# Newton's steps of the layer norm in the batch passes: from VectorE to Pool

## The chip, the core and the metric

The kernel runs on one core of a Trainium2 chip. The core has a matrix engine (TensorE, PE in the profile), a vector engine (VectorE, DVE), an activation engine (ScalarE, ACT), a general engine (GpSimd, POOL) and an engine that issues the transfers here (SyncE, SP). The engines run their own instruction streams side by side and wait for one another through semaphores. The metric is the device time of one execution in microseconds. The kernel before takes 328.29 us, the median of three runs (327.77 to 330.49).

## What is computed

Two layers of a decoder step for four batch entries (B = 4, one token each, D = 512). Each layer is an attention block over a cached K and V (32 query heads, 8 K/V heads, 4096 positions, head size 128) and a gated block (F = 1792), each behind a layer norm and with a residual. Both layers use the same caches and weights, all bfloat16.

```python
def _layernorm(x, axis=-1, eps=1e-5):
    m = jnp.mean(x, axis=axis, keepdims=True)
    v = jnp.var(x, axis=axis, keepdims=True)
    return (x - m) / jnp.sqrt(v + eps)

def _A_ref(x, k_cache, v_cache, wq, wo):
    q = (x @ wq).reshape(B, 1, 32, 128).transpose(0, 2, 1, 3)
    k = jnp.repeat(k_cache, 4, axis=1); v = jnp.repeat(v_cache, 4, axis=1)
    p = softmax(jnp.einsum("bhqd,bhkd->bhqk", q, k) * 128 ** -0.5)
    o = jnp.einsum("bhqk,bhkd->bhqd", p, v)
    return o.transpose(0, 2, 1, 3).reshape(B, 1, 4096) @ wo

def _B_ref(x, w_gate, w_up, w_down):
    h = sigmoid(x @ w_gate) * (x @ w_up)
    return h @ w_down

x = A_x
for _ in range(2):
    x = x + _A_ref(_layernorm(x), ...)
    x = x + _B_ref(_layernorm(x), ...)
```

## The kernel before

**Blocks and slots.** The caches are read in blocks of 1 MB, one per layer, batch entry and K/V head, for K and V alike. Twelve slots in SBUF hold them. SP issues a load as soon as the planned next load has a free slot (`pump`, L332), and some blocks of layer 0 are kept for layer 1. Freed slots, by the last product that reads a block, therefore set when the loads start.

**Steps.** The main loop (L1146) takes two heads per step, 32 steps in all, and each step also does the V products of the step before: scores on PE (`scores`, L910), the row maximum on DVE (`smax`, L926), its spread over the rows on PE (`spread_max`, L935), the bias on DVE (L945) and the exponential on ACT (L953), the transposes of the next K blocks on DVE (`k_turn`, L893), the V products on PE (`pv`, L1018), their scaling on DVE (L1046), the turn of the probabilities (`ptrans`, L970 on PE and 16 copies of L1002 on ACT), and the output projection (`wo_pair`, L1062 on PE, L1076 on DVE). Every engine takes its instructions in the order in which the program hands them out; there is no planner, and `_Sched` (L34) only adds the semaphore waits from the names that each instruction reads and writes. A wait is also set between two dependent instructions of one engine.

**Passes.** When a batch entry has finished its attention of layer 0, a pass takes it through the gated block and on to the query of layer 1 (`pass_steps`, L859). There are four, one per entry, and the list `places` (L1102) says after which part of which step each of the 19 parts of a pass is handed out. A pass has two halves, and each begins with a layer norm: `ln_a` (mean, centred x), `ln_b_sum` (sum of squares on PE, L550), `ln_b_rs` (L555).
- `ln_b_rs` reduces the sum on DVE (L558, from PSUM), forms variance plus eps (L565, `vpe`) and a first guess of the inverse root from its bits (L570, `y0i`), and for one entry calls `newton_one` (L503): three Newton steps, each two instructions on one column of 128 rows (L507 and L515), the last of which writes `rs`.
- First half: gate row on PE (`gate_row`, L709), `gate_tanh` (the scale `rsg` from `rs` on DVE, L721; the tanh on ACT, L726), `up_row` (L738), `up_gate` (copy on ACT, L749; product on DVE, L751), `h_turn` (L762 on PE, L768 on DVE), `down` (L828) and `down_add` (L841, L851).
- Second half: query rows on PE (`q_row`, L779, twice), `q_out(0)` (ACT, L792, scaled by `rs`), `q_half(0)` on PE (L809), `q_out(1)` (DVE, L799, scaled by `rs`), `q_turn` (L809, L818), `q_spread` (L620 on PE, L631 on ACT).

In DVE's order, Newton's steps of the first half stand between the row maximum (L926) and the bias (L945) of the same step, the gate's scale right behind that bias and ahead of a K transpose; Newton's steps of the second half stand ahead of the row maximum of their step.

**Pool.** Pool forms the query blocks of each step (`q_blocks`, L645), one product of 128 x 128 elements, and nothing else after the start. For the first heads of a batch entry in layer 1, `q_blocks` comes after the end of that entry's pass.

The start (L1086) and the end (L1194) do the layer norm for all four entries at once; there `ln_b_rs` calls `newton_many`.

Of the kernel before, what the change touches and what calls it, by code (L numbers as in the profile page):

```python
# [7 lines left out]
ALU = mybir.AluOpType  # L8
# [107 lines left out]
def bass_interleave_layers__gqa_block_cached__glu_gated_glu__decode_kernel(  # L116
# [41 lines left out]
    S = _Sched()  # L158
# [40 lines left out]
    lnsum, lnsq, vpe, nt_a, nt_b, nt_c, nt_y, rs = [newt[:, i, :] for i in range(8)]  # L199
# [154 lines left out]
    def dve(fn, reads=(), writes=()):  # L354
        return S.inst("dve", fn, reads=reads, writes=writes)

    def act(fn, reads=(), writes=()):
        return S.inst("act", fn, reads=reads, writes=writes)

    S.dma("sp", lambda e: e.dma_start(x_io[0:Bn, :], A_x.rearrange("b s d -> (b s) d")), "xin", writes=["row0"])  # L360
    for k in range(KD):
# [4 lines left out]
            writes=[f"wq{k}"],  # L366
# [6 lines left out]
        reads=["ones_f"],  # L373
        writes=["pe0"],
    )
    dve(lambda e: e.transpose(pidx[:, :], iota_f[:, 0:32]), writes=["pe0"])
    for a in range(4):
# [5 lines left out]
            reads=["pe0"],  # L383
            writes=[f"ident{a}"],
# [5 lines left out]
    for k in range(KD):  # L390
# [12 lines left out]
        reads=["M0"],  # L403
        writes=[f"x{b}" for b in range(Bn)],
# [62 lines left out]
    def ln_a(b0, nb):  # L467
# [22 lines left out]
            writes=["xc"],  # L490
        )
        act(
            lambda e: e.activation(xc_bf[:, :, 0:nb], xc_sb[:, :, 0:nb], ACTF.Copy),
            reads=["xc"],
# [8 lines left out]
    def newton_one(y0):  # L503
        y, yk = y0, "y0i"
        for it, three in enumerate((3.0, 12.0, 768.0)):
            dve(
                (lambda y: lambda e: e.scalar_tensor_tensor(  # L507
                    out=nt_a[:, 0:1], in0=y, scalar=vpe[:, 0:1], in1=y, op0=ALU.mult, op1=ALU.mult
                ))(y),
                reads=[yk, "vpe"],  # L510
                writes=["nt_a"],
            )
            z, zk = ((nt_b[:, 0:1], "nt_b"), (nt_c[:, 0:1], "nt_c"), (rs[:, 0:1], "rs"))[it]
            dve(
                (lambda y, z, three: lambda e: e.scalar_tensor_tensor(  # L515
                    out=z, in0=nt_a[:, 0:1], scalar=-three, in1=y, op0=ALU.add, op1=ALU.mult
                ))(y, z, three),
                reads=[yk, "nt_a"],
                writes=[zk],
            )  # L520
            y, yk = z, zk

    def newton_many(y0, nb):
        y, yk = y0, "y0i"
        for it, three in enumerate((3.0, 12.0, 768.0)):
            dve(
                (lambda y: lambda e: e.tensor_tensor(nt_a[:, 0:nb], y, y, ALU.mult))(y),
                reads=[yk],
                writes=["nt_a"],
            )  # L530
            dve(
                lambda e: e.tensor_tensor(nt_y[:, 0:nb], nt_a[:, 0:nb], vpe[:, 0:nb], ALU.mult),
                reads=["nt_a", "vpe"],
                writes=["nt_y"],
            )
            z, zk = ((nt_b[:, 0:nb], "nt_b"), (nt_c[:, 0:nb], "nt_c"), (rs[:, 0:nb], "rs"))[it]
            dve(
                (lambda y, z, three: lambda e: e.scalar_tensor_tensor(
                    out=z, in0=nt_y[:, 0:nb], scalar=-three, in1=y, op0=ALU.add, op1=ALU.mult
                ))(y, z, three),  # L540
                reads=[yk, "nt_y"],
                writes=[zk],
            )
            y, yk = z, zk
# [10 lines left out]
    def ln_b_rs(nb):  # L555
        M = M_ps[1]
        dve(
            lambda e: e.tensor_reduce(  # L558
                lnsq[:, 0:nb], M[:, 32:32 + KD * nb].rearrange("p (k b) -> p b k", k=KD), AX.X, ALU.add
            ),  # L560
            reads=["M1"],
            writes=["lnsq"],
        )
        dve(
            lambda e: e.tensor_scalar(vpe[:, 0:nb], lnsq[:, 0:nb], inv_d, eps, op0=ALU.mult, op1=ALU.add),  # L565
            reads=["lnsq"],
            writes=["vpe"],
        )
        dve(
            lambda e: e.tensor_scalar(  # L570
                y0i[:, 0:nb], vpe[:, 0:nb].bitcast(dt.int32), -0.5, RSQRT_MAGIC, op0=ALU.mult, op1=ALU.add
            ),
            reads=["vpe"],
            writes=["y0i"],
        )
        y0 = y0i[:, 0:nb].bitcast(dt.float32)
        if nb == 1:
            newton_one(y0)
        else:
            newton_many(y0, nb)  # L580

    def ln_b(nb):
        ln_b_sum(nb)
        ln_b_rs(nb)
# [29 lines left out]
    def q_spread(b0, nb):  # L614
        N = HQ * nb
        fns = []
        for t in range(NT4):
            for a in range(4):
                fns.append(
                    (lambda t, a: lambda e: e.matmul(  # L620
                        M_ps[1][32 * a:32 * a + 32, t * N:(t + 1) * N],
                        lhsT=ident_bf[:, bass.ds(64 * (t // 2) + t % 2, 32, step=2)],
                        rhs=qT_sb[:, 0:N],
                        start=True,
                        stop=True,
                    ))(t, a)
                )
        S.group("pe", fns, reads=["qT"] + IDENT, writes=["M1"])
        for bi in range(nb):
            act(  # L630
                (lambda bi: lambda e: e.activation(  # L631
                    qc_sb[:, b0 + bi, :, :, :],
                    M_ps[1][:, 0:NT4 * N].rearrange("p (t u r b) -> p u t r b", t=NT4, u=HKV, r=REP)[:, :, :, :, bi],
                    ACTF.Copy,
                ))(bi),
                reads=["M1"],
                writes=[f"qc{b0 + bi}"],
            )
# [16 lines left out]
    def gate_up(nb, which):  # L655
# [14 lines left out]
        if which == 0:  # L670
            dve(
                lambda e: e.tensor_tensor(
                    gs_sb[:, 0:KF * nb].rearrange("p (k b) -> p k b", k=KF),
                    M[:, 64:64 + KF * nb].rearrange("p (k b) -> p k b", k=KF),
                    bc(rs[:, 0:nb], KF, nb),
                    ALU.mult,
                ),
                reads=["M0", "rs"],
                writes=["pe0"],
            )  # L680
            act(
                lambda e: e.activation(t_sb[:, 0:KF * nb], gs_sb[:, 0:KF * nb], ACTF.Tanh, scale=0.5 * RS),
                reads=["pe0"],
                writes=["pe0"],
            )
        else:
            dve(
                lambda e: e.scalar_tensor_tensor(
                    out=hT_bf[:, :, 0:nb],
                    in0=t_sb[:, 0:KF * nb].rearrange("p (k b) -> p k b", k=KF),  # L690
                    scalar=1.0,
                    in1=M[:, 64:64 + KF * nb].rearrange("p (k b) -> p k b", k=KF),
                    op0=ALU.add,
                    op1=ALU.mult,
                ),
                reads=["pe0", "M1"],
                writes=["qT"],
            )
# [18 lines left out]
        S.group("pe", fns, reads=["xcb"] + wkeys["wg"], writes=["M0"])  # L717

    def gate_tanh():
        dve(  # L720
            lambda e: e.tensor_scalar(rsg, rs[:, 0:1], 0.5 * RS, None, op0=ALU.mult),  # L721
            reads=["rs"],
            writes=["rsg"],
        )
        act(
            lambda e: e.activation(M_ps[0][:, :], M_ps[0][:, :], ACTF.Tanh, scale=rsg),  # L726
            reads=["rsg"],
            writes=["M0"],
        )
# [129 lines left out]
    def pass_steps(b0):  # L859
        return [  # L860
            lambda: ln_a(b0, 1),
            lambda: ln_b_sum(1),
            lambda: ln_b_rs(1),
            gate_row,
            gate_tanh,
            up_row,
            up_gate,
            h_turn,
            lambda: down(b0, 1),
            lambda: down_add(b0, 1),  # L870
            lambda: ln_a(b0, 1),
            lambda: ln_b_sum(1),
            lambda: ln_b_rs(1),
            lambda: q_row(0),
            lambda: q_out(0),
            lambda: q_row(1),
            lambda: q_out(1),
            q_turn,
            lambda: q_spread(b0, 1),
        ]  # L880
# [380 lines left out]
```

## Time and profile before

| | |
|---|---|
| median of three runs | 328.29 us (327.77 to 330.49) |
| the profiled execution | 326.9 us, of which the profiled span is 325.1 us |
| PE busy | 224.6 us (69%) |
| DVE busy | 190.3 us (59%), 443 instructions |
| ACT busy | 146.0 us (45%) |
| POOL busy | 12.8 us (4%), 36 instructions |
| read from memory | 120.85 MB, 372 GB/s over the span |
| mean granted PE clock | 0.71 of full speed |

A span is the time between the first and the last instruction of one profiled execution; 1.8 us of that execution lie around it. A group row gives the line, the engine, the operation, what is written and read with its shape, the count, the busy time, the mean duration of one instruction, and how long its engine sat idle just before such instructions and for whom. A row of the chain of work that ended last gives a start, a duration and the work that the end depended on in that stretch. A window row gives, for one stretch of time, the busy share and number of instructions of PE, PE's weight loads, DVE, ACT and POOL, the granted clock, the busy share of the transfer engines and what they moved.

### The profile page before, as it was taken

The page shows a single profiled execution, that of the slowest core. Times are in us where ns is not written, and L with a number is a line of the kernel's source. Part 1 is how long each engine was busy: PE and PEld are TensorE (multiplying, and loading weights), DVE is VectorE, ACT ScalarE, POOL GpSimd, SP SyncE. Part 2 cuts the span into 40 slices and gives each one's busy share as a digit, 9 for nine tenths or more (in the row PEclk, how much of TensorE's full clock was granted, in tenths as well). Part 3 has the DMA queues.
Part 4 walks back from the last instruction along what each step waited for, and adds up shares of the span by engine and source line. Part 5 has one row for each costly group of instructions (what it writes and reads, how often), then busy time and mean ns, then how long its engine had stood idle before and what let it go on. Part 6 is the DMA issues. An engine that isn't in the chain of part 4 may idle for free.

```text
span 325.1 us, 10423 instructions
## 1 busy us (share of the span) xinstructions
PE 224.6 (69%) x4408; PEld 156.7 (48%) x4408; DVE 190.3 (59%) x443; ACT 146.0 (45%) x600; POOL 12.8 (4%) x36
## 2 busy tenths in 40 slices
PE   1345514322298988859699885979977778988975
PEld 1313312221166556636556653665555556455865
DVE  6387333331566566876544986664996567475443
ACT  1005412303046367654637664462766454377620
POOL 0000000000000000000001000000100000010000
PEclk9999999999999955555675555566555557655555
DMA  7999999999999899999989999999999999899700
GB/s 280 428 419 410 400 404 402 401 382 392 401 414 391 347 409 422 421 418 361 382 299 390 420 422 420 418 423 416 417 418 421 417 357 386 331 390 415 296 2 5
DMA packets 22526, 121.53 MB, mean 374 GB/s; under 512 B 1992, under 2 KB 7888, under 8 KB 8912
## 3 DMA queue, kind: packets, MB, share of 16 engines
q1 hardware_dynamic: 22480, 120.86, 92.5%
q8 instruction: 35, 0.57, 0.7%
q14 instruction: 11, 0.09, 0.1%
HBM read 120.85 MB, written 0.00 MB: 372 GB/s over the span
## 4 chain that ended last, share of the span: by engine, by line
DMA 32%; PE 27%; issue 20%; SPq 11%; DVE 8%; POOL 0%; ACT 0%; DVEq 0%; POOLq 0%
DMA slot<-in_A_v_cache_dram 32%; PE O_ps L1018 8%; SPq L352 6%; PE S_ps L910 6%; SPq L338 4%; DVE slot L893 4%; PE MS L935 2%; PE O_ps L1062 2%; PE MS L977 2%; PE M_ps L828 1%; DVE small L926 1%; PE PT L970 1%; PE M_ps L779 1%; PE M_ps L661 1%; PE M_ps L473 1%
## 5 line engine op out<-in xcount | busy, mean ns | idle before, releaser
L893 DVE STREAM_TRANSPOSE slot<-slot 128x2048 f32<-128x2048 f32 (+1 forms) x63 | 114.8, 1822 | 41.8 <-DMA slot<-in_A_k_cache_dram 41.8
L1002 ACT ACTIVATE pT<-PT 32x64 bf16<-32x64 f32 x504 | 108.5, 215 | 61.4 <-PE PT L970 49.8
L1018 PE MATMUL O_ps<-pT,slot 128*128 128x4 bf16 x2048 | 63.0, 166 | 37.5 <-DMA slot<-in_A_v_cache_dram 36.8
L1018 PEld LDWEIGHTS O_ps<-pT,slot 128*128 128x128 bf16 x2048 | 64.4, 105 | 41.0 <-DMA slot<-in_A_v_cache_dram 40.3
L910 PE MATMUL S_ps<-slot,qz 128*16 128x512 bf16 x512 | 59.2, 610 | 3.3 <-POOL qz L645 2.7
L953 ACT ACTIVATE pe<-S_ps,small 128x512 bf16<-128x512 f32 x32 | 22.0, 687 | 69.3 <-issue 36.4
L935 PE MATMUL MS<-valid_f,small 128*128 128x64 f32 x64 | 20.2, 415 | 32.2 <-DVE small L926 32.2
L935 PEld LDWEIGHTS MS<-valid_f,small 128*128 128x128 f32 x64 | 14.7, 286 | 45.5 <-DVE small L926 42.2
L1062 PEld LDWEIGHTS O_ps<-oT,wo 128*128 128x128 bf16 x640 | 19.3, 105 | 12.9 <-issue 12.4
L926 DVE TENSOR_REDUCE small<-S_ps 128x1 f32<-128x512 f32 x32 | 21.2, 663 | 7.0 <-PE S_ps L910 7.0
L645 POOL TENSOR_TENSOR qz<-qc,small 128x128 bf16<-128x128 bf16 x32 | 12.6, 401 | 281.1 <-ACT qc L631 148.2
L910 PEld LDWEIGHTS S_ps<-slot,qz 128*16 128x16 bf16 x512 | 12.3, 108 | 22.5 <-issue 17.5
L1062 PE MATMUL O_ps<-oT,wo 128*128 128x2 bf16 (+1 forms) x640 | 20.2, 165 | 1.2 <-issue 0.9
L1046 DVE TENSOR_TENSOR oT<-O_ps,rden 128x8 bf16<-128x8 f32 x32 | 5.2, 164 | 23.2 <-PE O_ps L1018 21.4
L977 PE MATMUL MS<-head_f,small 128*128 128x8 f32 x64 | 17.6, 348 | 0.0
L977 PEld LDWEIGHTS MS<-head_f,small 128*128 128x128 f32 x64 | 16.1, 309 | 0.0
L985 DVE RECIPROCAL rden<-MS 128x8 f32<-128x8 f32 x32 | 6.6, 206 | 13.2 <-PE MS L977 13.2
L970 PE MATMUL PT<-ident_bf,pe 128*128 128x64 bf16 x128 | 11.7, 230 | 1.7 <-ACT pe L953 1.7
L945 DVE CUSTOM_DVE_ANT_0 junk<-MS,mask_f,small 128x64 bf16<-128x64 f32 x32 | 8.5, 265 | 7.3 <-PE MS L935 7.3
L779 PE MATMUL M_ps<-wq,xc_bf 128*1 128x512 bf16 x128 | 12.6, 563 | 0.0
L473 PE MATMUL M_ps<-xT,small 128*128 128x4 f32 (+1 forms) x20 | 5.8, 362 | 5.6 <-DVE xT L851 2.2
L550 PEld LDWEIGHTS M_ps<-sq,small 128*128 128x128 f32 x20 | 5.0, 312 | 8.4 <-issue 6.8
(79 smaller groups left out, 144.1 us busy)
## 6 DMA issues: line engine op xcount, KB each, us to landing
slot<-in_A_v_cache_dram SPq DMA_DIRECT2D x53, 1024.0 KB, 10.9
slot<-in_A_k_cache_dram SPq DMA_DIRECT2D x49, 1024.0 KB, 11.5
wq<-in_A_wq_dram SPq DMA_DIRECT2D x4, 1024.0 KB, 7.8
wo<-in_A_wo_dram SPq DMA_DIRECT2D x8, 512.0 KB, 16.2
wg<-in_B_w_gate_dram SPq DMA_DIRECT2D x4, 448.0 KB, 14.1
wu<-in_B_w_up_dram SPq DMA_DIRECT2D x4, 448.0 KB, 14.5
wd<-in_B_w_down_dram SPq DMA_DIRECT2D x2, 896.0 KB, 16.5
row<-in_A_x_dram SPq DMA_DIRECT2D x1, 4.0 KB
```

The costliest lines, as they stand in the source:

```text
L352: S.dma("sp", (lambda dst, src: lambda e: e.dma_start(dst, src))(dst, src), f"d{s}", writes=[f"s{s}"])
L779: (lambda k, st: lambda e: e.matmul(M_ps[h][32 * st:32 * st + 1, :], lhsT=xc_bf[:, k, 0:1], rhs=wv[:, k, h, :, st, :], start=(k == 0), sto ...
L893: dve(lambda e: e.transpose(kf, kf), writes=[f"s{st}"])
L910: (lambda t, b2, e_, c, r0, ul: lambda e: e.matmul(S_ps[p][r0:r0 + 4 * REP, :], lhsT=qz_sb[p][:, ul, t, :, :].rearrange("p a r -> p (a r)" ...
L926: lambda e: e.tensor_reduce(rm_sb[p], S_ps[p][:, :], AX.X, ALU.max),
L935: lambda e: e.matmul(MS[:, 0:16 * REP], lhsT=rm_sb[p].broadcast_to([P, P]), rhs=valid_f[:, :], start=True, stop=True),
L953: lambda e: e.activation(pe_sb[p].rearrange("p j m -> p (j m)"), S_ps[p][:, :], ACTF.Exp, bias=nm_sb[p], scale=exp_scale, accum_out=sm_sb[ ...
L970: (lambda j: lambda e: e.matmul(PT[:, j * 64:(j + 1) * 64], lhsT=pe_sb[p][:, j, :], rhs=valid_bf, start=True, stop=True))(j)
L977: lambda e: e.matmul(MS[:, 64:64 + 2 * REP], lhsT=sm_sb[p].broadcast_to([P, P]), rhs=head_f[:, :], start=True, stop=True),
L1002: (lambda dst, frm: lambda e: e.activation(dst, frm, ACTF.Copy))(dst, frm),
L1018: (lambda x, c, j: lambda e: e.matmul(O_ps[p][:, ul * REP:(ul + 1) * REP], lhsT=vv[:, x * JG + c * 4 + j, :], rhs=pT_sb[p][:, x, j, 2 * ul ...
L1062: (lambda c, r: lambda e: e.matmul(O_ps[p][:, 64 + 2 * c:64 + 2 * c + nb], lhsT=wo_sb[:, u * REP + r, c * P:(c + 1) * P], rhs=oT_sb[n][:, ...
```

## The change

In the four passes, variance, first guess, Newton's six operations and the gate's scale are handed to Pool instead of DVE. DVE's `scalar_tensor_tensor` becomes Pool's `tensor_scalar` with the second tensor as a column scalar, so that each half step stays one operation. The reduce L558 stays on DVE, as do the layer norms of all four entries at the start and the end (`nb` is 4 there).

```diff
+    def pool(fn, reads=(), writes=()):
+        return S.inst("pool", fn, reads=reads, writes=writes)
+
...
     def newton_one(y0):
         y, yk = y0, "y0i"
         for it, three in enumerate((3.0, 12.0, 768.0)):
-            dve(
-                (lambda y: lambda e: e.scalar_tensor_tensor(
-                    out=nt_a[:, 0:1], in0=y, scalar=vpe[:, 0:1], in1=y, op0=ALU.mult, op1=ALU.mult
+            pool(
+                (lambda y: lambda e: e.tensor_scalar(
+                    nt_a[:, 0:1], y, y, vpe[:, 0:1], op0=ALU.mult, op1=ALU.mult
                 ))(y),
...
-            dve(
-                (lambda y, z, three: lambda e: e.scalar_tensor_tensor(
-                    out=z, in0=nt_a[:, 0:1], scalar=-three, in1=y, op0=ALU.add, op1=ALU.mult
+            pool(
+                (lambda y, z, three: lambda e: e.tensor_scalar(
+                    z, nt_a[:, 0:1], -three, y, op0=ALU.add, op1=ALU.mult
                 ))(y, z, three),
...
-        dve(
+        eng = pool if nb == 1 else dve
+        eng(
             lambda e: e.tensor_scalar(vpe[:, 0:nb], lnsq[:, 0:nb], inv_d, eps, op0=ALU.mult, op1=ALU.add),
...
-        dve(
+        eng(
             lambda e: e.tensor_scalar(
                 y0i[:, 0:nb], vpe[:, 0:nb].bitcast(dt.int32), -0.5, RSQRT_MAGIC, op0=ALU.mult, op1=ALU.add
             ),
...
     def gate_tanh():
-        dve(
+        pool(
             lambda e: e.tensor_scalar(rsg, rs[:, 0:1], 0.5 * RS, None, op0=ALU.mult),
```

## The prediction

> **What bounds the kernel now.** I read the chain that ended last first, since busy shares mix stages with different limits. Its totals, then pieces of it in order of time (start us, us, what):
>
> ```profile
> DMA 32%; PE 27%; issue 20%; SPq 11%; DVE 8%; POOL 0%; ACT 0%; DVEq 0%; POOLq 0%
> ```
> ```profile
> 245.53 16.36 DMA slot<-in_A_v_cache_dram
> 261.93 1.01 PE O_ps L1018 x32
> ...
> 272.98 0.58 DVE row L751
> 273.70 0.25 PE M_ps L762 x4
> ...
> 279.49 3.39 PE M_ps L779 x31
> 282.88 0.19 PE M_ps L809 x4
> ...
> 322.74 0.68 DVE row L1215
> ```
>
> Up to 261.9 us the chain keeps coming back to V blocks: the cache stream sets the time, and a delay in computing counts only if it starves that stream. After 261.9 no transfer is left on the chain: the fourth pass (264 to 286 us) and all behind it are computing, so a delay there reaches the end whole.
>
> The other passes start at about 92, 148 and 206 us. Whether they starve the stream is read from one-microsecond windows (last two columns: DMA share, GB/s):
>
> ```profile
> 107.00:108.00 1.00, 1.00 (x10) 0.55 (x14) 0.47 (x3) 0.00 (x0) 0.00 (x0) 1.00 0.70 172
> 108.00:109.00 1.00, 1.00 (x20) 0.33 (x16) 0.85 (x5) 0.00 (x0) 0.00 (x0) 1.00 0.51 131
> ...
> 164.00:165.00 1.00, 1.00 (x14) 0.41 (x17) 0.62 (x4) 0.00 (x0) 0.00 (x0) 0.50 0.50 98
> ...
> 222.00:223.00 1.00, 1.00 (x16) 0.32 (x12) 0.90 (x5) 0.10 (x1) 0.00 (x0) 0.50 1.02 426
> ```
>
> Passes 1 and 2 already empty the stream (172, 131 and 98 GB/s against 418 when full); pass 3 does not, and the chain then waits 16.4 us for a V block, so whatever pass 3 gains or loses is swallowed.
>
> Last, the rows that price the change (xcount | busy us, mean ns | idle before it) and the wait behind it:
>
> ```profile
> L507 DVE SCALAR_TENSOR_TENSOR newt<-newt 128x1 f32<-128x1 f32 x24 | 5.3, 219 | 0.9
> ...
> L515 DVE SCALAR_TENSOR_TENSOR newt<-newt 128x1 f32<-128x1 f32 x24 | 3.8, 159 | 0.8
> ...
> L602 DVE SCALAR_TENSOR_TENSOR qT<-M_ps,newt 128x128 bf16<-128x128 f32 x1 | 0.3, 252 | 0.0
> ...
> L370 DVE MEMSET small<- 128x1 f32 x1 | 0.1, 59 | 0.8 <-PEq L1246 0.8
> ```
> ```profile
> L645 POOL TENSOR_TENSOR qz<-qc,small 128x128 bf16<-128x128 bf16 x32 | 12.6, 401 | 281.1 <-ACT qc L631 148.2 <-PE S_ps L910 123.9 <-ACT pT L1002 8.9
> ...
> L1246 POOL MEMSET const-float32-0.0<- 128x1 f32 x1 | 0.1, 99 | 0.2 <-issue 0.2
> ```
> ```profile
> ACT row L792 <- DVE newt L515: 12.5, 4, 3.1
> ```
>
> **What moves.** In the order of instructions DVE goes from 422 to 354 and Pool from 40 to 108: 17 per pass, 8 in each half plus the gate's scale, so the change does what it says. Nothing else changes place, no DMA and no SP instruction. Pool's next product (L645) stood behind the end of the pass anyway and stays there. On ACT the tanh (L726) now waits for Pool's scale; queued behind it are the up copy (L749) and the 16 copies of L1002. In the second half ACT's q copy (L792) waits for Pool's rs, and behind it on PE stand L809, the spread (L935) and the V products.
>
> **Price of a Pool step.** No row shows Pool working on one column. From below, Pool's memset of 128x1 takes 99 ns; from above, its product of 128x128 takes 401 ns, with 128 times the elements but no column scalar. Two pairs of rows compare the engines: 401 against 252 ns (L602, as many elements) is 1.59, 99 against 59 ns (memsets) is 1.68. I take 1.6 times the DVE duration: 246 ns for each of L565 and L570 (154 on DVE), 350 for L507, 254 for L515, 238 for L721 (149). Every step waits for the one before it on its own engine; on DVE that leaves 35 to 40 ns between them, and Pool starts 70 ns after its releaser (ACT's qc ends at 170.00, L645 starts at 170.07). I take 70 ns. A DVE transpose does not slow Pool: the product at 184.27 lies inside a transpose (182.52 to 184.78) and takes 0.40 us like the rest.
>
> [...]
>
> **Newton's result (rs).** On DVE it is ready 1.73 us after the reduce L558 (96.15 to 97.88, and 107.59 to 109.32). On Pool: 0.07 to start, 2 x 0.246 + 3 x 0.350 + 3 x 0.254 = 2.30 of work, 7 x 0.07 = 0.49 between: 2.86, which is 1.13 later; with ACT starting 0.07 instead of 0.03 after it, **1.17 us later**.
>
> **First half (tanh).** Scale and tanh: 2.86 + 0.07 + 0.24 + 0.07 = 3.24 us after L558 instead of 2.74 (pass 4: 268.72 to 271.46), 0.50 late. DVE is free sooner: in pass 4 L945 can start near 269.7, when its product is there, not at 270.40, so exp and transpose come 0.7 earlier. That relief ends at the tanh.
> - Pass 1: nothing. The copy L749 could start at 99.96 but waits for the up products until 100.13.
> - Pass 2: nothing. L762 stands behind V products whose block landed at 157.57.
> - Pass 3: 0.26 late, swallowed.
> - Pass 4: today L751 waits for the transpose that ends at 272.98, not for ACT. Then: tanh 271.96, copy 272.53 to 273.13, L751 273.16 to 273.81, L762 0.15 later at 273.96, not 273.70: **+0.26**.
>
> **Second half (q).** L792 comes 1.17 later; what PE is doing covers part of it.
> - Pass 1 runs at full clock: PE is done with L779 at 109.80 and starts L809 at 110.09, when L792 ends. All 1.17 shows on PE. The two blocks asked for at 106.97 and 107.35 start to flow at about 108.8 and last 5.0 us, to 113.9; the next is asked for at 111.49 and flows some 1.8 later, at 113.3. That margin of 0.6 goes first: **+0.57**.
> - Pass 2: L792 ends at 166.89, L809 starts at 167.17: 0.23 covered by L779. The stream refills at 165.7 and lasts to 170.7, the next block at 168.56 + 1.85 = 170.4: margin 0.3. 1.17 - 0.23 - 0.3: **+0.64**.
> - Pass 3: 0.75 covered, 0.42 left, swallowed.
> - Pass 4: PE at half clock works on L779 until 282.8, L792 ends at 282.14: 0.63 covered, **+0.54**. Were the clock full here, as in pass 1, this cover would be gone and it would be 1.17.
>
> **Sum**: 0.26 + 0.57 + 0.64 + 0.54 = 2.0 us on a profiled execution of 326.9 (span 325.1): 328.9. The median shown is 328.29, 1.4 above that execution, so **330.3 us**, 0.6% more. One per cent, 3.3 us, is about what a measurement of this kernel tells from no change.
>
> **Bounds.** At the memset's 99 ns rs is ready after 0.07 + 0.80 + 0.49 = 1.36 us, sooner than on DVE; then pass 4 gains in its first half alone, 0.29 us (L762 follows the V products that end at 273.41), and I get 328.0. At 401 ns for every step rs is 2.07 late and the scale 1.56: 1.47, 1.54 and 1.44 in the second halves of passes 1, 2 and 4; 0.85, 0.4 and 1.32 in the first halves: 7.0 us, 335.3. My value lies nearer the upper row, because these steps read operands as that row does and a memset does not.
>
> **Rivals.**
> - *A column scalar costs Pool as much as a second tensor* (place: the six steps of L507 and L515 in each half): 401 ns each, as L645 has it, the other two at 246. Then rs comes 1.77 late and the tanh 1.10: pass 1 0.43 + 1.17, pass 2 1.24, pass 4 0.86 + 1.14: 4.8 us, **333.1**, slower by 1.5%. Between the forecast's mean for these steps (302 ns) and 401 it passes 1% at about 350 ns. For it: no Pool row has a column scalar, and on DVE the second one costs 60 ns (219 against 159). Against it: the two ratios above, with one column to work on. Steps dearer still, the first two and the scale at 401 as well, give the upper end.
> - *Pool's small steps are cheap*, below 0.22 us a step with the wait: no loss, L762 of pass 4 comes 0.29 earlier, **328.0**. For it: four memsets start only 0.03 us apart. Against: they read nothing.
> - *The freed DVE time counts*: 2 x 1.73 + 0.15 = 3.6 us of DVE per pass, 14 in all, if it were on the path; a quarter gives **324.7**. Against it: outside pass 4 nothing on the chain waits for the DVE work behind Newton's steps, and in pass 4 only the 0.29 above. For it: DVE is 59% busy and transposes stand on the chain elsewhere.
>
> **Chances.** The forecast (328.6 to 331.5) 0.33, the dear column scalar (331.6 to 333.7) 0.29, dearer still 0.13, cheap 0.19, freed DVE 0.06. So faster by over 1% 0.06, within 1% 0.52, slower by over 1% 0.42. The range, 327.8 to 334.2, leaves out the last case and most of the dearest.
>
> **What the changed profile would show.** Right: Pool rows of 0.25 to 0.35 us at one column; some 2.9 us from L558 to the end of rs; L945 about 0.5 us earlier against L558; ACT waiting for Pool before the q copy; PE's gap before L809 of pass 1 grown from 0.3 to about 1.4 us; the stream's hole near 107 us no deeper but a new one near 114. Wrong: Pool steps above 0.40 us; a hole in pass 3; a pass 4 that keeps its length though Pool is slow; V waits after 286 us, which would mean that the stream sets the end after all.

## The result and the profile after

| | before | after |
|---|---|---|
| median of 13 runs each | 328.02 us (326.71 to 330.49) | 330.78 us (329.59 to 332.36) |
| ratio, 95% interval | | 1.0089 [1.0063, 1.0114] |
| the profiled execution | 326.9 us, span 325.1 | 330.1 us, span 328.3 |
| DVE busy, instructions | 190.3 us, 443 | 178.9 us, 375 |
| POOL busy, instructions | 12.8 us, 36 | 31.2 us, 104 |

The change costs 2.9 us (2.1 to 3.7 by the interval), 0.9% (0.6 to 1.1). The forecast was 330.3 us, 2.0 more than before, just under that interval. The kernel is slower; the middle value stays below the 1% bound, which the interval just passes. The change handed 68 instructions to an engine that takes 1.23 to 1.67 times as long for them (below), and in the second half of each pass ACT waits for the last of them.

In the kernel after, the lines have moved by three to four: Newton's steps are L510 and L518 (L507 and L515 before), the reduce is L561 (L558), variance and guess L569 and L574 (L565 and L570), the scale L725 (L721), the tanh L730 (L726), PE's query rows L783 (L779), the q copies L796 and L803 (L792 and L799), the first turn of q L813 (L809), the V products L1022 (L1018).

**Price of a step.** The groups of Pool in the kernel after, columns as in the rows of the kernel before (xcount | busy us, mean ns | idle before it):

```profile
L510 POOL TENSOR_SCALAR newt<-newt 128x1 f32<-128x1 f32 x24 | 8.2, 341 | 2.4
L518 POOL TENSOR_SCALAR newt<-newt 128x1 f32<-128x1 f32 x24 | 6.4, 265 | 2.5
L569 POOL TENSOR_SCALAR newt<-newt 128x1 f32<-128x1 f32 x8 | 1.5, 190 | 92.3 <-DVE newt L561 92.3
L574 POOL TENSOR_SCALAR newt<-newt 128x1 int32<-128x1 int32 x8 | 1.5, 190 | 0.7
L725 POOL TENSOR_SCALAR small<-newt 128x1 f32<-128x1 f32 x4 | 0.9, 216 | 0.4
```

Against the same steps on DVE that is 341 to 219 ns (1.56), 265 to 159 (1.67), 190 to 154 (1.23) and 216 to 149 (1.45). Two column scalars cost most, one less, none least. The idle time (2.4 us over 24) is the 0.10 us that each step waits for the one before it on its own engine. The starts alone say the same: the next step starts 0.29 us after L574, 0.36 after L518 and 0.44 to 0.45 after L510.

**Who waits.** Waits of the kernel after (us in all, times, longest):

```profile
ACT row L796 <- POOL newt L518: 18.1, 4, 4.5
...
PE M_ps L813 <- ACT row L796: 4.2, 4, 1.8
...
ACT M_ps L730 <- POOL small L725: 3.2, 4, 0.8
```

Before, ACT waited 12.5 us in all for DVE ahead of the q copy; now it is 18.1, for Pool, and PE waits 4.2 us behind it, in all four passes, where the kernel before has 0.3 us in one.

**Where it sits in a pass.** Pass 1 in the timeline of the kernel after (start us, us; in brackets the engine's wait and what ended it):

```profile
107.76 3.58 PE L783 MATMUL M_ps<-wq,xc_bf 128*1 128x512 bf16 x32
107.87 0.16 DVE L561 TENSOR_REDUCE newt<-M_ps 128x1 f32<-128x4 f32 x1 [1.77 <-PE M_ps L553]
...
108.12 0.19 POOL L569 TENSOR_SCALAR newt<-newt 128x1 f32<-128x1 f32 x1 [8.29 <-DVE newt L561]
...
110.74 0.27 POOL L518 TENSOR_SCALAR newt<-newt 128x1 f32<-128x1 f32 x1
111.10 0.69 ACT L796 ACTIVATE row<-M_ps,newt 128x512 bf16<-128x512 f32 x1 [4.52 <-POOL newt L518]
...
111.85 0.26 PE L813 MATMUL M_ps<-ident_bf,row 128*128 128x4 bf16 x4 [0.50 <-ACT row L796]
```

The reduce ends at 108.03, rs is ready at 111.01, 2.98 us later, and PE takes the turn L813 3.82 us after the reduce. It is 3.82 in every one of the four passes: Pool's chain alone sets it. PE's gap is only 0.50 us, because its query rows took 3.58 us here. In the timeline of the kernel before they took 2.48:

```profile
107.32 2.48 PE L779 MATMUL M_ps<-wq,xc_bf 128*1 128x512 bf16 x32
```

**The chain that ended last** in the kernel after, its totals and the pieces that answer to those shown of before:

```profile
PE 33%; DMA 31%; SPq 11%; DVE 11%; ACT 5%; POOL 5%; issue 4%; ACTq 0%; DVEq 0%; POOLq 0%
```
```profile
223.63 0.35 POOL newt L510
...
247.87 15.35 DMA slot<-in_A_v_cache_dram
263.27 1.02 PE O_ps L1022 x32
...
268.50 6.71 DMA slot<-in_A_v_cache_dram
275.26 1.02 PE O_ps L1022 x32
...
282.85 0.35 POOL newt L510
...
284.91 0.28 POOL newt L518
285.27 0.70 ACT row L796
...
325.92 0.68 DVE row L1219
```

POOL went from 0% to 5% of the chain. Where PE's query rows (279.49, 3.39 us) and L809 stood, there now stand Newton's steps on Pool and the q copy that waits for them. The totals of the two chains can't be compared further, for the chain of the kernel before has two long stretches of "issue", in which nothing that the profile shows was waited for, and they hide passes 2 and 3:

```profile
141.19 28.85 issue
...
197.28 30.00 issue
```

Nor does a place on the chain prove a cost: the chain of the kernel after also holds Pool's steps of pass 3 (223.63 above), where the experiments find that the change costs nothing.

**The stream.** Windows of the kernel after (last two columns: DMA share, GB/s), then the one of the kernel before that was not shown:

```profile
107.00:108.00 1.00, 1.00 (x10) 0.61 (x10) 0.13 (x2) 0.00 (x0) 0.00 (x0) 1.00 0.72 303
108.00:109.00 1.00, 1.00 (x13) 0.28 (x9) 0.63 (x2) 0.00 (x0) 0.69 (x3) 1.00 0.86 172
...
114.00:115.00 1.00, 0.71 (x25) 0.58 (x22) 0.42 (x3) 0.64 (x4) 0.28 (x1) 1.00 0.68 197
...
223.00:224.00 1.00, 1.00 (x16) 0.34 (x12) 0.57 (x1) 0.00 (x0) 0.72 (x3) 0.50 1.04 434
```
```profile
114.00:115.00 1.00, 1.00 (x35) 0.57 (x24) 1.00 (x1) 0.90 (x5) 0.40 (x1) 1.00 0.98 369
```

The hole near 107 us is no deeper (303 and 172 GB/s against 172 and 131), a new one stands at 114 us (197 against 369), and pass 3 has none: 434 GB/s while Pool works on its rs.

**Where the 3.2 us between the two profiled executions lie.** The start of each pass (the first product of `ln_a`) and the marks within pass 4, after minus before:

| mark | before, us | after, us | difference | added since the mark above |
|---|---|---|---|---|
| pass 1 starts | 92.10 | 92.47 | 0.37 | 0.37 |
| pass 2 starts | 148.43 | 150.10 | 1.67 | 1.30 |
| pass 3 starts | 206.10 | 207.43 | 1.33 | -0.34 |
| pass 4 starts | 264.67 | 266.01 | 1.34 | 0.01 |
| pass 4, second reduce ends | 279.69 | 282.19 | 2.50 | 1.16 |
| pass 4, first turn of q | 282.82 | 286.01 | 3.19 | 0.69 |
| end of the span | 325.1 | 328.3 | 3.2 | 0.0 |

0.37 us is there before the first changed instruction, and 1.16 lies in a stretch where the experiments below find no cost. One pair of executions therefore doesn't settle the terms; the medians of the experiments do it better.

### The profile page after: what moved, and what is told of

It reads as the page before. It is cut to its first block, busy times and chain, and to the rows that moved or that the text cites. A ratio compares the mean times of both kernels' runs of the same rounds, so it can differ in the third digit from the quotient of the medians.

```text
span 328.3 us, 10419 instructions
## 1 busy us (share of the span) xinstructions
PE 228.7 (70%) x4408; PEld 158.3 (48%) x4408; DVE 178.9 (55%) x375; ACT 145.9 (44%) x600; POOL 31.2 (9%) x104
## 4 chain that ended last, share of the span: by engine, by line
PE 33%; DMA 31%; SPq 11%; DVE 11%; ACT 5%; POOL 5%; issue 4%; ACTq 0%; DVEq 0%; POOLq 0%
DMA slot<-in_A_v_cache_dram 31%; PE O_ps L1022 11%; PE S_ps L914 7%; SPq L352 6%; DVE slot L897 6%; SPq L338 4%; PE O_ps L1066 3%; ACT pT L1006 3%; PE MS L939 3%; PE MS L981 2%; POOL newt L510 2%; DVE small L930 2%; PE PT L974 2%; PE M_ps L476 2%; POOL newt L518 2%
## 5 line engine op out<-in xcount | busy, mean ns | idle before, releaser
L1022 PE MATMUL O_ps<-pT,slot 128*128 128x4 bf16 x2048 | 63.0, 167 | 33.0 <-DMA slot<-in_A_v_cache_dram 32.4
L1022 PEld LDWEIGHTS O_ps<-pT,slot 128*128 128x128 bf16 x2048 | 65.0, 106 | 37.5 <-DMA slot<-in_A_v_cache_dram 36.7
L914 PE MATMUL S_ps<-slot,qz 128*16 128x512 bf16 x512 | 60.0, 618 | 3.0 <-POOL qz L649 2.4
L939 PE MATMUL MS<-valid_f,small 128*128 128x64 f32 x64 | 20.9, 427 | 30.7 <-DVE small L930 30.6
L939 PEld LDWEIGHTS MS<-valid_f,small 128*128 128x128 f32 x64 | 15.2, 296 | 44.1 <-DVE small L930 40.5
L649 POOL TENSOR_TENSOR qz<-qc,small 128x128 bf16<-128x128 bf16 x32 | 12.5, 398 | 167.7 <-PE S_ps L914 122.2
L914 PEld LDWEIGHTS S_ps<-slot,qz 128*16 128x16 bf16 x512 | 12.4, 109 | 22.6 <-issue 18.1
L783 PE MATMUL M_ps<-wq,xc_bf 128*1 128x512 bf16 x128 | 12.1, 544 | 0.0
L803 DVE TENSOR_SCALAR row<-M_ps,newt 128x512 bf16<-128x512 f32 x4 | 3.0, 752 | 14.3 <-PE M_ps L813 14.3
L796 ACT ACTIVATE row<-M_ps,newt 128x512 bf16<-128x512 f32 x4 | 2.7, 687 | 18.1 <-POOL newt L518 18.1
```

The costliest lines, as they stand in the source:

```text
L914: (lambda t, b2, e_, c, r0, ul: lambda e: e.matmul(S_ps[p][r0:r0 + 4 * REP, :], lhsT=qz_sb[p][:, ul, t, :, :].rearrange("p a r -> p (a r)" ...
L939: lambda e: e.matmul(MS[:, 0:16 * REP], lhsT=rm_sb[p].broadcast_to([P, P]), rhs=valid_f[:, :], start=True, stop=True),
L1022: (lambda x, c, j: lambda e: e.matmul(O_ps[p][:, ul * REP:(ul + 1) * REP], lhsT=vv[:, x * JG + c * 4 + j, :], rhs=pT_sb[p][:, x, j, 2 * ul ...
```

## The experiments

The theory: the time is lost where rs of the **second** half comes late, by what PE's query rows do not cover, in passes 1, 2 and 4; pass 3 is swallowed by the stream. Rivals: the first half counts as well; Pool costs something by being used, whatever waits for it; the stream swallows passes 1 and 2 too.

### Rs late by a known amount, one pass at a time

The kernel before, Newton's steps on DVE, with ten copies of rs onto itself on Pool behind them, in the second half of one pass. A copy takes 0.22 us and they stand 0.29 apart, so rs comes 2.9 us later. Nothing is left out.

```diff
+    def slow(b):
+        if b not in (0,):          # 0, 1, 2 or 3: the pass
+            return
+        for _ in range(10):
+            pool(lambda e: e.tensor_scalar(rs[:, 0:1], rs[:, 0:1], 1.0, None, op0=ALU.mult),
+                 reads=["rs"], writes=["rs"])
...
-            lambda: ln_b_rs(1),
+            lambda: (ln_b_rs(1), slow(b0)),
```

> The kernel before with ten Pool copies (rs times 1.0, each waiting for the one before) behind Newton's steps in the second half of pass 1 alone; the output stays the same. Ten steps of about 0.28 us make rs 2.85 us later. My theory (a late q copy shows on PE, and a pass costs the end what it starves the stream of beyond its margin, 0.6 us here): +2.2 us. Rival (everything ahead of pass 4 is swallowed by the waits for V blocks): 0. Rival (the chain is computing throughout): +2.85.

> The same ten Pool copies in pass 2 alone. My theory: 2.85 less 0.23 covered by PE less 0.3 of the stream's margin: +2.3 us. Rival (swallowed): 0. Rival (computing throughout): +2.6.

> The same ten Pool copies in pass 3 alone. My theory: the stream has blocks in stock through pass 3 and the chain waits 16 us for V blocks behind it, so 0 (within 0.5). Rival (computing throughout): 2.85 less 0.75 covered by PE, +2.1 us.

> The same ten Pool copies in pass 4 alone. My theory: nothing behind pass 4 waits for a transfer, so 2.85 less 0.63 covered by PE at half clock: +2.2 us. Rival (the stream sets the end after all, and has stock): near 0.

| late in | median, us | before, us | ratio, 95% | difference, us |
|---|---|---|---|---|
| pass 1 | 330.89 | 327.80 | 1.0088 [1.0064, 1.0113] | +2.9 (2.1 to 3.7) |
| pass 2 | 331.14 (4 runs) | 327.80 | 1.0114 [1.0049, 1.0180] | +3.7 (1.6 to 5.9) |
| pass 3 | 328.13 | 327.80 | 1.0005 [0.9977, 1.0032] | +0.2 (-0.8 to 1.0) |
| pass 4 | 330.25 | 327.80 | 1.0065 [1.0036, 1.0094] | +2.1 (1.2 to 3.1) |

Passes 1, 2 and 4 pay for a late rs; for pass 3 the times show no cost. Pass 3 of its own run, in the timeline:

```profile
222.67 2.84 POOL L781 TENSOR_SCALAR newt<-newt 128x1 f32<-128x1 f32 x10 [25.55 <-DVE newt L518]
225.60 0.69 ACT L805 ACTIVATE row<-M_ps,newt 128x512 bf16<-128x512 f32 x1 [6.11 <-POOL newt L781]
...
226.35 0.26 PE L822 MATMUL M_ps<-ident_bf,row 128*128 128x4 bf16 x4 [2.27 <-ACT row L805]
```

PE stands still for 2.27 us ahead of L822 (L809 before), and yet the median moves by 0.2 us only. The windows of that run say why, and those of the run with pass 1 late show the contrast:

```profile
225.00:226.00 1.00, 0.00 (x0) 0.00 (x0) 0.00 (x0) 0.40 (x1) 0.42 (x2) 1.00 1.08 451
...
228.00:229.00 1.00, 1.00 (x45) 0.95 (x42) 0.19 (x2) 0.59 (x3) 0.00 (x0) 0.50 0.96 320
229.00:230.00 1.00, 0.83 (x10) 0.60 (x11) 0.38 (x2) 0.86 (x4) 0.70 (x2) 0.50 0.89 320
```
```profile
112.00:113.00 1.00, 0.00 (x0) 0.00 (x0) 0.00 (x0) 0.39 (x1) 0.42 (x2) 1.00 1.00 426
...
114.00:115.00 1.00, 1.00 (x46) 1.00 (x43) 0.84 (x4) 0.24 (x1) 0.00 (x0) 1.00 0.00 0
115.00:116.00 1.00, 1.00 (x45) 0.95 (x41) 0.18 (x2) 0.63 (x3) 0.00 (x0) 0.56 0.22 49
```

While PE is idle the stream runs full in both (451 and 426 GB/s). The difference comes behind it. In both passes two blocks were asked for ahead of the idle time (220.24 and 220.62, 107.25 and 107.63), and the next one 7.1 us later, after some two us in which no V product freed a slot. In pass 1 the stream had run low before those two flowed (164 GB/s at 108 us), and it stands empty from 114 us on (0, then 49 GB/s). In pass 3 blocks asked for earlier were still on their way (401 to 442 GB/s from 220 to 224 us), and the stream only thins, to 320.

It does thin: from the start of pass 3 to that of pass 4 this execution takes 59.52 us, and the other thirteen that were profiled take 58.52 to 58.70, the kernel after among them (58.58). So pass 3 swallows the delay of the change whole, but not quite all of ten copies.

In pass 4 Pool's copies stand on the chain that ended last of that run:

```profile
282.18 0.17 DVE newt L518
282.43 0.22 POOL newt L781
282.72 0.22 POOL newt L781
```

### One half alone

Second halves alone on Pool (the scale on DVE), then first halves and scale alone on Pool:

```diff
-        eng = pool if nb == 1 else dve
+        eng = pool if half == 2 else dve     # half == 1 in the other kernel
...
-            newton_one(y0)
+            newton_one(y0, eng)              # on DVE: scalar_tensor_tensor, as before
...
-        pool(
+        dve(                                 # the gate's scale; pool in the other kernel
```

> Only the second halves on Pool; the first halves and the gate's scale stay on DVE. My theory: rs in the second half, 1.2 us late, is most of the loss: 0.57 + 0.64 + 0.54 = +1.8 us. Rival (the tanh behind Pool's scale is most of it, as the profiled execution with its pass 4 suggests, 1.1 us late at L766): +0.7.

> Only the first halves and the gate's scale on Pool. My theory: passes 1 to 3 hide the late tanh, pass 4 shows 0.3 to 0.5 us of it: +0.4 us. Rival (first half is the larger part): +1.5 to +2.

| on Pool | median, us | before, us | ratio, 95% | difference, us |
|---|---|---|---|---|
| second halves | 330.31 | 327.97 | 1.0071 [1.0047, 1.0095] | +2.3 (1.5 to 3.1) |
| first halves and scale | 327.89 | 327.97 | 0.9988 [0.9970, 1.0005] | -0.4 (-1.0 to 0.2) |

The loss is in the second halves. The first halves cost nothing that could be measured and gain at most 1 us, while +0.4 had been expected. That also speaks against a cost of Pool's mere use, since this kernel has 9 of the 17 moved instructions of each pass; the kernel with all 17 on Pool and one Newton step, below, shows it better. The two parts add up to 1.9 us where all of it costs 2.9, each known to about 0.8 either way. The chain of the first-halves kernel shows what covers the later tanh in pass 4:

```profile
266.51 6.77 DMA slot<-in_A_v_cache_dram
273.33 0.96 PE O_ps L1026 x32
274.73 1.60 PE M_ps L836 x56
```

PE's V products (L1026 here) wait for a block that lands at 273.28, and the down products follow. The same is seen in the kernel after, pass 4, in its timeline:

```profile
271.50 0.28 DVE L949 CUSTOM_DVE_ANT_0 junk<-MS,mask_f,small 128x64 bf16<-128x64 f32 x1 [1.44 <-PE MS L939]
...
273.45 0.66 ACT L730 ACTIVATE M_ps<-M_ps,small 128x512 f32<-128x512 f32 x1 [0.80 <-POOL small L725]
...
275.26 1.02 PE L1022 MATMUL O_ps<-pT,slot 128*128 128x4 bf16 x32 [1.28 <-DMA slot<-in_A_v_cache_dram]
```

The tanh comes 3.38 us after the reduce (270.07), 0.64 later than before, but PE waits for the V block until 275.26 whatever ACT does.

### Fewer Newton steps

One step instead of three, on Pool and on DVE (`newton_many` too), with `RS` set to suit; and two steps with the second halves alone on Pool. These leave out two, and one, of the three Newton steps, so rs is less exact: worked out from the constants of the code, the first guess is off by up to 3.4%, and rs by up to 0.18% after one step and 0.0005% after two. (The 0.2% that the first expectation below gives to the guess is that of one step.)

```diff
-    RS = -1.0 / 8192.0
+    RS = -0.5                                # two steps: 1.0 / 16.0
...
-        for it, three in enumerate((3.0, 12.0, 768.0)):
+        for it, three in enumerate((3.0,)):  # two steps: (3.0, 12.0)
```

> The changed kernel with one Newton step in place of three (the first guess is good to 0.2%, one step makes it better than bfloat16; the factor RS follows; the steps at the start and the end of the kernel are shortened too). Pool's rs is then ready some 1.4 us after the reduce, sooner than DVE's 1.73. My theory (Pool costs only by lateness): no loss is left, 0 to -0.5 us against before. Rival (Pool at work beside DVE, PE and the transfers costs by itself): half or more of the +2.8 us stays.

> The kernel before with one Newton step in place of three, all on DVE: rs is ready 0.83 us after the reduce. My theory: there is little to win, 0.3 us in pass 1 (swallowed) and 0.3 us in pass 4: -0.3 us, not to be told from no change. Rival (DVE's Newton time is on the path in every pass, 0.9 us a half): -3 us or more.

> Second halves on Pool, as in the run of the second half alone, with two Newton steps in place of three (RS follows): rs is ready 0.81 us sooner, 2.2 us after the reduce, and the q half could start about 3.0 us after it, where with DVE's three steps it starts 2.5 to 3.25 us after it, as PE ends its q rows. My theory (PE's own q rows and the stream's margins cover the rest): 0 to +0.5 us against before. Rival (each microsecond of Pool costs in proportion, 2.3 us for 1.25 us of lateness): +0.8 us. Rival (Pool in the second half costs by itself): +2.3 us stays.

| | median, us | before, us | ratio, 95% | difference, us |
|---|---|---|---|---|
| Pool, one step | 327.75 | 327.97 | 0.9972 [0.9950, 0.9994] | -0.9 (-1.6 to -0.2) |
| DVE, one step | 328.13 | 327.97 | 1.0002 [0.9979, 1.0026] | +0.1 (-0.7 to 0.9) |
| second halves on Pool, two steps | 327.86 | 327.06 | 1.0018 [0.9992, 1.0045] | +0.6 (-0.3 to 1.5) |

With all of it on Pool and one step, the loss is gone. ACT's wait ahead of the q copy then ends with PE's query rows and no longer with rs, in the Pool kernel as in the DVE kernel (waits of the two):

```profile
ACT row L796 <- PE M_ps L783: 12.4, 4, 3.1
```
```profile
ACT row L792 <- PE M_ps L779: 12.4, 4, 3.1
```

This is the floor under the pass: PE's own rows. From there a shorter rs wins nothing, as the DVE kernel shows (+0.1), and Pool costs what it runs past that floor: +2.3 with the three steps of the second halves, nothing with one step. The run with two steps (+0.6) lies between, as it should, but its interval holds both the 0 to 0.5 of this account and the 0.8 of a cost in proportion to the lateness, so it doesn't decide between them; it excludes that the 2.3 stays.

### A version that might beat the kernel before

One step, first halves and scale on Pool, second halves on DVE; run twice, the second time beside a repeat of the one-step Pool kernel:

```diff
-        eng = pool if nb == 1 else dve
+        eng = pool if half == 1 else dve
...
-        for it, three in enumerate((3.0, 12.0, 768.0)):
+        for it, three in enumerate((3.0,)):
```

> The best of the parts: first halves and the gate's scale on Pool, second halves on DVE, one Newton step in place of three in both. My theory: rs is never what PE or ACT waits for, and DVE is freed where it held the bias and a transpose: -0.3 to -0.9 us, not better than one step on Pool throughout by more than 0.5 us. Rival (the second half on DVE is worth something of its own once the steps are short): a further -0.5 us or more.

> The mixed kernel (first halves and scale on Pool, second halves on DVE, one step) beside it. If its +1.5 us is real, it comes again, and stands at least 1 us behind one step on Pool throughout; if it came from the chip, both lie within 0.7 us of each other.

> One Newton step on Pool once more, now beside the mixed kernel on one chip, since the first run of it (0.9 us faster than before) and the mixed kernel's (1.5 us slower) come from two chips and no reason for such a difference is known. If the parts add up as the runs of the halves say: 0 to -0.9 us against before. If the single runs are only good to 1.5 us between chips: anything from -0.5 to +1.

| | median, us | before, us | ratio, 95% | difference, us |
|---|---|---|---|---|
| mixed | 328.71 | 327.06 | 1.0045 [1.0025, 1.0066] | +1.5 (0.8 to 2.2) |
| mixed, again | 328.27 | 327.86 | 1.0005 [0.9983, 1.0028] | +0.2 (-0.6 to 0.9) |
| Pool, one step, again | 327.69 | 327.86 | 0.9992 [0.9965, 1.0018] | -0.3 (-1.1 to 0.6) |

A miss: -0.3 to -0.9 was expected of the mixed kernel, and it came out at +1.5 on one chip and +0.2 on another. Beside the one-step Pool kernel it is 0.6 us slower, within the 0.7 that was expected if the first figure came from the chip. The intervals hold for one chip; from chip to chip the difference of this kernel repeated only to 1.3 us. That holds for the experiments above too, which were made on three chips: the 2 to 3 us of a late second half stand, the steps of some tenths between experiments don't. None of these versions is shown to beat the kernel before. Why the mixed kernel was slower on the first chip stays open.

## Why the prediction was right, and where it was off

**Right: the place and the sign.** A late rs is paid in the second halves of passes 1, 2 and 4 and swallowed in pass 3. The ten copies, a dose of lateness in one pass at a time, show each of the four, the one-half experiment shows that the second halves carry the loss, and the one-step kernel on Pool shows that it is the lateness and not the engine.

**Right: the price.** Ready 2.86 us after the reduce by the forecast, 2.98 by the trace. The terms: 350 ns forecast and 341 measured for L507, 254 and 265 for L515, 246 and 190 for the first two, 238 and 216 for the scale; 70 ns between steps was too little, (2.98 - 2.20) / 8 = 0.10 us is what the trace has. It was luck in part that the sum came so near: one ratio of 1.6 stood for rows that have 1.23 to 1.67, and the cheap first two steps made up for half of the longer waits between steps. The tanh came at 3.38 us (3.24 forecast). So the rival of the dear column scalar (401 ns each) falls, and so does the cheap one.

**Fallen: the freed DVE time.** First halves and scale on Pool free 1.9 us of DVE in each pass (1.73 and 0.15) and gain 0.4 us in all by the middle value, 1.0 at most; two Newton steps less on DVE gain nothing (+0.1).

**Wrong: "Pass 1 runs at full clock", as something that stays.** In the profiled execution of before it did: the full clock is on record there from 108.5 us, and the 32 query-row products took 2.48 us. But it belongs to that execution and not to the pass, and the clock column doesn't tell. Two windows of the kernel after, in which PE's query rows run in pass 1 and in pass 4 (the column ahead of the last two is the granted clock):

```profile
108.10:111.50 3.40, 3.25 (x32) 0.84 (x24) 0.53 (x1) 0.40 (x1) 2.20 (x8) 1.00 0.91 318
282.00:285.40 3.40, 3.40 (x32) 0.86 (x32) 0.76 (x2) 0.13 (x1) 2.20 (x8) 0.50 0.82 287
```

Granted 1.00 in one and 0.50 in the other, and the 32 products take 3.58 us in both. In the kernel after the first change of the clock on record is later than this (111.6 us), and the column has 1.00 up to it. So PE's gap in pass 1 was 0.50 us and not the 1.4 that I had put down as a sign; the cover is not the same from one execution to the next either. From the end of the second reduce to PE's first turn of q, us, in the profiled execution of each kernel that has the three steps on DVE (the late pass of a dose kernel left out), and in the Pool kernels:

| kernel | pass 1 | pass 2 | pass 3 | pass 4 |
|---|---|---|---|---|
| before | 2.50 | 2.73 | 3.25 | 3.13 |
| pass 1 late | - | 2.52 | 3.25 | 3.25 |
| pass 2 late | 3.19 | - | 3.10 | 2.96 |
| pass 3 late | 3.25 | 2.50 | - | 2.50 |
| pass 4 late | 3.05 | 3.25 | 2.55 | - |
| first halves on Pool | 3.24 | 2.50 | 3.01 | 2.50 |
| **mean of these** | 3.05 | 2.70 | 3.03 | 2.87 |
| after | 3.82 | 3.82 | 3.82 | 3.82 |
| second halves on Pool | 3.85 | 3.85 | 3.85 | 3.85 |
| the same, two steps | 3.04 | 3.04 | 3.25 | 3.03 |
| late by ten copies | 5.49 | 5.48 | 5.49 | 5.48 |

On DVE the time is 2.50 where rs sets it and up to 3.25 where PE's rows do, which take from 2.31 to 3.58 us. Where the clock is on record over them they are the shorter the more of it was granted: in passes 2 to 4 of before 3.07, 3.58 and 3.46 us at 0.61, 0.50 and 0.54, in those of after 2.31, 2.65 and 3.58 us at 0.81, 0.71 and 0.50. The profiled execution of before had an unusually fast pass 1 (2.50) and a slow pass 4 (3.13).

**Mis-sized: the lateness, and the cover of pass 4.** PE's turn comes 1.32 us later than the earliest on DVE (3.82 against 2.50) and not 1.17, in every pass. In pass 4 the forecast counted on 0.63 us of cover, the part of the delay in which PE is still busy with its rows; the mean of the table leaves 0.37 (2.87 less 2.50), so that pass 4 comes to 0.95 and not 0.54.

**Not settled: the margins of the stream.** The forecast took 0.6 us off in pass 1 and 0.3 in pass 2. Without them, and with the means of the table, passes 1, 2 and 4 give 0.77 + 1.12 + 0.95 = 2.8 us for the kernel after (2.9 measured) and 0.80 + 1.15 + 0.98 = 2.9 for the second halves alone (2.3, 1.5 to 3.1). With two steps, the larger of 3.04 and each entry, less the mean, gives 0.10 + 0.38 + 0.23 = 0.7 (0.6 measured). The doses give 2.4, 2.8 and 2.6 (2.9, 3.7 and 2.1), each inside its interval. The forecast counted otherwise, from the 2.50 us at which rs sets the turn, and took its margin off that; for ten copies in pass 1 that is 2.99 - 0.6 = 2.4, the same. Only a margin on top of the mean cover, 1.8, lies outside the 2.1 to 3.7. So the times can't tell the two ways of counting apart, but they forbid taking off both.

The stream itself shows a margin in pass 1. What it moved in the 5 us that start 20 us after the start of the pass (112.10 to 117.10 in before):

| kernel | turn of q in pass 1, us after the reduce | GB/s |
|---|---|---|
| before | 2.50 | 393 |
| pass 4 late | 3.05 | 383 |
| pass 2 late | 3.19 | 408 |
| first halves on Pool | 3.24 | 397 |
| pass 3 late | 3.25 | 395 |
| after | 3.82 | 346 |
| second halves on Pool | 3.85 | 333 |
| pass 1 late | 5.49 | 210 |

Turns of 2.50 to 3.25 us make no difference there (395 GB/s in the mean). For the three later ones the bytes missing against that mean are worth 0.6, 0.7 and 2.2 us at 418 GB/s, which is 0.6 to 0.8 less than these turns come after 2.50: so much of a delay costs the stream nothing. That is the margin that the forecast named, and its 0.57 for pass 1 agrees with the 0.6 of the kernel after. Between the two profiled executions pass 2 did start 1.30 us later against pass 1, but that pair is no measure: from start to start pass 1 takes 56.33 to 57.29 us in the first five kernels of this table, and before has the shortest. Whether pass 2 has its 0.3 is open: its dose interval is too wide, and the pair of profiled executions gained 0.34 us over that pass.

**Wrong: +0.26 in the first half of pass 4.** It rested on V products that end at 273.41, before the later up product; the block that they wait for lands later in other executions. L945 came 0.25 us earlier against the reduce (1.43 us instead of 1.68), not about 0.5, since it then waits for PE's spread (L939). The first-halves kernel measured -0.4 us (-1.0 to 0.2), which leaves little room for the 0.26. Of the 1.16 us that this stretch took more in the profiled execution of after, 1.10 stands ahead of the turn in the gated block, where the V block landed 6.7 us after its request instead of 5.2. The run with pass 4 late, whose code is that of before up to that point, has 6.77 us on its chain there, so the change need not be its cause.

**Too narrow: "After 261.9 no transfer is left on the chain".** The chain of the kernel after itself has a V block in pass 4 (268.50, 6.71 us, above), and so have seven others of the fourteen. Behind pass 4 five have one: first halves on Pool (283.91, 7.34 us), pass 3 late (284.73, 6.61), second halves on Pool (286.81, 6.84), pass 2 late (286.96, 7.50) and the mixed kernel (286.17, 6.56). So in some executions the stream still sets the time after pass 4, and I had named such waits after 286 us as a sign against the forecast. The profiled execution of the kernel after has none there, and a late rs in pass 4 costs 2.1 us by its dose, within what the delay of 2.6 allows. How much of it the stream swallows in such executions is open.

**The sum** came out 0.9 us low. The lateness, 0.15 more in each of three passes, and the cover of pass 4, 0.26 less, make 0.7 of that; the first half's 0.26 was too much and hid some of it. Some 0.4 us are left, less than the interval can tell, and no run says where they lie. The forecast's own second halves without margins, 1.17 + 0.94 + 0.54 = 2.65, come within 0.3 us of the result, but that is luck: the 1.17 of pass 1 has no cover at all, and the table has 0.55 there in the mean.

## What to carry to other kernels

A chain of tiny dependent steps, moved to an engine that took 1.23 to 1.67 times as long for each, cost its lateness here only where something waited for its last result and nothing else was late there: the four first halves lost nothing that could be measured (-0.4 us, -1.0 to 0.2), and of the second halves the one with loads enough in hand lost nothing by the change (pass 3, 58.58 us from its start to that of pass 4 against 58.57). Before counting on cover, look whether the covering work keeps its length: PE rows that change with the granted clock (2.31 us at 0.81, 3.58 at 0.50) covered between 0 and 0.75 us of the same delay, so one profiled execution gives one draw of it. And look at the stream behind a delay, not only during it: in passes 1 and 3 it ran full while PE stood idle (426 and 451 GB/s), and what told them apart was how much was still on its way when the next load was asked for. A cover and a margin can overlap: taking off both, the mean cover and the margin of pass 1, gives a time outside the one measured.

## What was not expected of the hardware

- In the two profiled executions of before and after the full clock is on record in pieces of 3.4 and 6.8 us, and half of it between them: in before at 108.5 to 115.4, 152.9 to 156.3, 166.6 to 170.0 us and four times more, in after at 111.6 to 115.0 and 166.2 to 173.1 and twice more. The places differ from one execution to the next: the 32 query-row products of pass 1 took 2.48 us in the profiled execution of before, 2.35 in one other and 3.17 to 3.58 in the remaining twelve. Over 13 runs of after a higher mean granted clock goes with a shorter time (correlation -0.65; 329.63 us at 0.709, 332.26 at 0.683).
- Pool's price for one column rose with the column scalars: 190 and 216 ns with none, 265 with one, 341 with two. Its product of two tensors of 128 columns took 398.
- A V block of pass 4 landed 5.2 us after its request in the profiled execution of before, 6.7 in that of after and 6.8 in the run with pass 4 late, where the code ahead of it is that of before.
